# Loads of wo's pages moved behind the last stack copy, five heads later, in an Infini-attention and token-mixer kernel

## The chip, the cores and the metric

The kernel runs on one core of a Trainium2 chip. A core has five engines, each of which takes its own instructions strictly in order: TensorE (PE; its weight loads are listed apart as PEld), VectorE (DVE), ScalarE (ACT), GpSimd (POOL) and SyncE (SP), which here issues nearly all DMAs. They wait for each other by semaphores. The metric is the device time of the program in microseconds; lower is better.

## The reference

Two blocks with conditioning from a vector c: an attention over four segments of 512 tokens with a memory carried from segment to segment, and a token-mixing MLP. Cut to what is computed:

```python
mod = (_silu(c) @ w_mod).reshape(c.shape[0], 6, 1, -1)      # sa, ca, ga, sb, cb, gb
h = _layernorm(x, axis=-1) * (1 + ca) + sa
x = x + ga * _A_ref(h, A_wq, A_wk, A_wv, A_wo, A_beta)
h = _layernorm(x, axis=-1) * (1 + cb) + sb
x = x + gb * _B_ref(h, B_w1, B_b1, B_w2, B_b2)

# _A_ref: 32 heads of 32, 4 segments of 512 tokens
for s in range(N):
    logits = jnp.einsum("bhqd,bhkd->bhqk", qs, ks) * scale + mask
    a_dot = jnp.einsum("bhqk,bhkd->bhqd", _softmax(logits, axis=-1), vs)
    pq = phi(qs)
    a_mem = einsum(pq, M) / (einsum(pq, z) + 1e-6)
    outs.append(g * a_mem + (1.0 - g) * a_dot)
    M, z = M + einsum(phi(ks), vs), z + sum(phi(ks))
return o @ wo                                                # (2048, 1024) @ (1024, 1024)

# _B_ref: layernorm, u = gelu(h^T w1 + b1), y = u w2 + b2, across the tokens
```

## The kernel before

Products in full precision are made of three reduced-precision ones: an operand is kept as a high and a low part (function `split`: ACT casts the high part, another engine subtracts for the low one). A *page* is one such operand of 128 partitions, two parts of 512 columns, 512 KB, and there are 16 page buffers, taken in turn.

**Attention.** An iteration t is one group of four heads in one segment; there are 32 (`NI`), first all groups for segments 0 and 1, then all groups for segments 2 and 3, alternating between the two. Iteration 30 is the last group in segment 2, iteration 31 in segment 3. The main loop runs over n, one head at a time, and each step calls, for different heads, `scores` (logits and exponentials of head n; matmuls `a0`, `a1`, `a2`, exponentials p, their low part by POOL), `maxima` (row maxima of head n + 3; matmuls `sx`, `sy`, `sz`, then a transpose `nmps`), `values` (head n - 2; twenty matmuls `pv`), and `project` for the piece m = n + 8 of an iteration: pieces 0 and 1 are keys and values (`nps`), piece 2 transposes the keys (`kps`), makes the queries (`qps`), and writes both split into `sg`. From `sg` and from the maxima, SP copies the operands of the scores into *stacks* `sk`: three copies a head (`sk<-sg`, lines 374 to 376, function `stack`), and later four small ones for two heads (`sk<-nt`, line 493). There are two sets of four stacks, used in turn by odd and even iterations. The head outputs are transposed (`ops`), copied to `ot` and stored to `oT`.

In the second half the 16 pages hold the normalised tokens of segments 2 and 3, eight each. The loads of the sixteen pages of wo go into the same buffers, so the first eight (`wo0_0` to `wo7_0`, the columns 0 to 511 of the output) have to wait until the queries of iteration 30 are made, the others (`wo0_1` to `wo7_1`) until those of iteration 31. Three of the latter are loaded within the output product instead (line 790).

**Output product.** `product(tt)`, for 128 tokens each, loads the head outputs (`otr`), splits them into `ots`, multiplies them with wo (48 matmuls `po`, 24 for each half, line 797), adds x and stores the sum to `x1d`. Products 0 and 1 come first, their halves in turn, then 2, 3, 4, 8, 9 and so on. The MLP follows: matmuls `mx` of line 927, nearly half of the chain of waits.

**Order.** The code is traced in the order written, and a scheduler then sets each engine's order by its own estimate of times; it starts the output product while the last heads are still under way, and places `po` matmuls between theirs. `tc.issue_after(ins)` is a bound on that order: an instruction under it on the same engine's queue stands behind `ins`. It adds no wait for the end of `ins`.

Of the kernel before, what the change touches and what calls it, by code (L numbers as in the profile page):

```python
# [7 lines left out]
F32 = mybir.dt.float32  # L8
# [33 lines left out]
def attention_and_mlp(ctx, tc, x, wq, wkv, wo, beta, w1, b1, w2, b2, c, wm_a, wm_b, out):  # L42
    nc = tc.nc
    V, A, G, T, SY = nc.vector, nc.scalar, nc.gpsimd, nc.tensor, nc.sync
# [9 lines left out]
    wos = dram.tile([NK, 2, P, 2, 512], F32, name="wos")  # L54
# [86 lines left out]
    def new_page(name):  # L141
        return page.tile([P, 2, 512], F32R, tag="page", bufs=16, name=name)
# [32 lines left out]
    def load_w(g, pr):  # L175
        res = W[pr, g] = {}
        for kind, part in (("v", 0), ("v", 1), ("q", 0)):
            load_part(g, pr, kind, part, res)
        if pr == 0:
            keep_w(g)  # L180
# [176 lines left out]
    def reload_h(seg, ct):  # L357
        pg = new_page(f"h{seg}_{ct}")
        SY.dma_start(pg.bitcast(F32), hT1[seg - 2, ct])
        hpages[seg, ct] = pg  # L360

    its = [(pr, g, 2 * pr + i) for pr in range(2) for g in range(NG) for i in range(2)]
    NI = len(its)
    st = {}

    last_sk, last_nt = {}, {}
# [131 lines left out]
    @contextmanager  # L498
    def behind(n, engines):

        with ExitStack() as s:
            for e in engines:
                if (n, e) in marks:
                    s.enter_context(tc.issue_after(marks[n, e].ins))
            yield
# [92 lines left out]
    def at(f, n):  # L598
        if 0 <= n < 4 * NI:
            f(n // 4, n % 4)  # L600
# [43 lines left out]
    wop = {}  # L644
# [46 lines left out]
    for n in range(-LEADS, 4 * NI + VL):  # L691
        at(scores, n)
        at(maxima, n + LEADS)
        with behind(n, "P" if n - VL >= 64 else ""):
            at(values, n - VL)
        m = n + LEADP
        if 0 <= m + 4 < 4 * NI:
            t = (m + 4) // 4
            if its[t][:2] not in W:
                with tc.issue_after(last_sk[t - 2 if t > 16 else 0, 3].ins):  # L700
                    load_w(its[t][1], its[t][0])
        if m >= 8:
            at(project, m)
        if 59 <= m < 67:
            seg, ct = 2 + (m - 59) // 4, 2 * ((m - 59) % 4)
            with ExitStack() as s:
                if seg == 3:
                    s.enter_context(tc.issue_after((last_sk[15, 3] if ct < 4 else last_nt[14, 3]).ins))
                reload_h(seg, ct)
                reload_h(seg, ct + 1)  # L710
        if 4 * NI - 5 <= m < 4 * NI + 3:
            i = m - 4 * NI + 5
            for c in (2 * (i % 4), 2 * (i % 4) + 1):
                wop[c, i // 4] = new_page(f"wo{c}_{i // 4}")
                if c < 5 or i < 4:
                    SY.dma_start(wop[c, i // 4].bitcast(F32), wos[c, i // 4])
        for f, engines in todo.pop(n, ()):
            with behind(n, engines):
                f()
# [427 lines left out]
```

## Time and profile before

| | |
|---|---|
| median of 3 runs | 2222.85 us (2221.31 to 2225.35) |
| profiled execution | 2224.45 us, its span 2222.7 us |
| mean granted TensorE clock | 0.997 |
| PE busy | 2184.5 us, 98% |
| attention's last heads with the output product between them | about 950 to 1046 us in the span |
| output product alone | to about 1151 us, then the MLP |

A busy TensorE is the sum of what its instructions cover; idle time is shown in brackets behind the row it precedes, with the releaser. Rows of one kind that follow each other are merged, so a row's length, divided by its count, tells the pace of one. On SP a row is the issue of DMAs, not their transfer.

### The profile page before, as it was taken

How to read it: one execution, taken by the hardware profiler on the slowest of the kernel's cores; microseconds unless marked ns; L12 is line 12 of the kernel's file. 1: busy time of each engine (PE TensorE's matmuls, PEld its weight loads, DVE VectorE, ACT ScalarE, POOL GpSimd, SP SyncE). 2: the span in 40 equal slices, each digit the busy share in tenths (PEclk: the TensorE clock that was granted, in tenths of full speed). 3: DMA queues.
4: the chain of work that ended last, by engine and by line, in shares of the span. 5: the costliest groups of instructions: out<-in, count | busy, mean ns of one | idle time of the engine just before them, and what ended most of it. 6: DMA issues, size and time to landing. Idle time of an engine off the chain costs nothing.

```text
span 2222.7 us, 38130 instructions
## 1 busy us (share of the span) xinstructions
PE 2184.5 (98%) x13786; PEld 1881.3 (85%) x13786; DVE 1673.2 (75%) x3762; ACT 1132.7 (51%) x2050; POOL 723.6 (33%) x831
## 2 busy tenths in 40 slices
PE   8999999999999999999999999999999999999999
PEld 5988998889999999888888888888888888888887
DVE  7677777767777677664858766888888887869687
ACT  5476777755666666654636533533334242424232
POOL 2165766656767677553002200033330000000000
PEclk9999999999999999999999999999999999999999
DMA  7656665587566665664754686655556541414134
GB/s 287 193 172 195 183 185 160 169 297 246 167 195 203 199 206 176 192 227 133 232 204 185 227 318 255 246 225 207 214 203 222 199 153 60 142 57 147 57 124 152
DMA packets 175184, 423.05 MB, mean 190 GB/s; under 512 B 17524, under 2 KB 71828, under 8 KB 166036
## 3 DMA queue, kind: packets, MB, share of 16 engines
q1 hardware_dynamic: 174996, 420.61, 57.4%
q8 instruction: 110, 1.80, 0.3%
q14 instruction: 78, 0.64, 0.1%
HBM read 244.62 MB, written 125.06 MB: 166 GB/s over the span
## 4 chain that ended last, share of the span: by engine, by line
PE 82%; DVE 6%; DMA 5%; ACT 3%; issue 1%; POOL 1%; SPq 1%; DVEq 0%; ACTq 0%
PE mx L927 47%; PE nps L192 10%; PE qps L200 7%; PE po L797 6%; PE pv L549 3%; DMA otr<-oT 1%; PE a L515 1%; DMA sk<-sg 1%; PE sz L478 1%; PE sx L478 1%; POOL p L531 1%; PE a L522 1%; PE sy L478 1%; PE a L518 1%; PE up L460 1%
## 5 line engine op out<-in xcount | busy, mean ns | idle before, releaser
L927 PE MATMUL mx<-bU,sp 128*128 128x512 f32 x2352 | 534.7, 389 | 1.0 <-DVE ac L934 0.9
L927 PEld LDWEIGHTS mx<-bU,sp 128*128 128x128 f32 x2352 | 441.1, 188 | 94.1 <-issue 1.3
L119 ACT CAST sp<-wr 128x384 fp32r<-128x384 f32 (+2 forms) x408 | 217.2, 545 | 433.0 <-PE mx L927 354.8
L192 PE MATMUL nps<-wv,h 128*128 128x256 f32 x3072 | 430.9, 283 | 1.1 <-DVE h L122 0.7
L927 PE MATMUL mx<-bA,sp 128*128 128x512 f32 x1764 | 430.5, 389 | 0.0
L531 POOL TENSOR_TENSOR p<-p,ph 128x640 f16<-128x640 f32 x256 | 377.7, 1476 | 121.7 <-ACT ph L529 116.8
L192 PEld LDWEIGHTS nps<-wv,h 128*128 128x128 f32 x3072 | 402.7, 190 | 8.8 <-DVE h L122 1.8
L927 PEld LDWEIGHTS mx<-bA,sp 128*128 128x128 f32 x1764 | 331.2, 188 | 68.7
L122 DVE TENSOR_TENSOR sp<-wr,sp 128x384 fp32r<-128x384 f32 (+2 forms) x408 | 259.1, 646 | 28.9 <-ACT sp L119 28.7
L934 DVE TENSOR_TENSOR ac<-mx,ac 128x512 f32<-128x512 f32 x280 | 189.4, 685 | 85.1 <-PE mx L927 84.5
L200 PE MATMUL qps<-h,wq 128*128 128x512 f32 x768 | 196.4, 399 | 0.0
L529 ACT CAST ph<-p 128x1280 f16<-128x1280 f32 x128 | 161.1, 1258 | 49.7 <-POOL p L527 49.2
L797 PE MATMUL po<-wo,ots 128*128 128x512 f32 x768 | 179.7, 391 | 1.4 <-ACT ots L119 1.4
L527 POOL TENSOR_SCALAR_AFFINE_SELECT p<-p 128x256 f32<-128x256 f32 x256 | 135.5, 535 | 119.9 <-ACT p L524 70.4
L797 PEld LDWEIGHTS po<-wo,ots 128*128 128x128 f32 x768 | 143.4, 188 | 31.2 <-ACT ots L119 1.8
L927 PE MATMUL mx<-bB,sp 128*128 128x512 f32 x588 | 164.0, 389 | 0.0
L200 PEld LDWEIGHTS qps<-h,wq 128*128 128x128 f32 x768 | 140.5, 189 | 27.1
L927 PEld LDWEIGHTS mx<-bB,sp 128*128 128x128 f32 x588 | 110.4, 188 | 22.9
L934 DVE TENSOR_TENSOR cc<-mx,cc 128x512 f32<-128x512 f32 x140 | 94.9, 684 | 41.7 <-PE mx L927 41.6
L480 DVE CUSTOM_DVE_ANT_0 sz<-sz,mask 128x512 f32<-128x512 f32 x128 | 89.2, 697 | 47.8 <-PE sz L478 46.9
L480 DVE CUSTOM_DVE_ANT_0 sx<-sx,mask 128x128 f32<-128x128 f32 (+1 forms) x256 | 93.3, 365 | 35.2 <-PE sx L478 31.5
L516 ACT ACTIVATE p<-a,shift 128x512 f32<-128x512 f32 x128 | 88.0, 688 | 43.6 <-PE a L515 39.6
(207 smaller groups left out, 3193.9 us busy)
## 6 DMA issues: line engine op xcount, KB each, us to landing
sk<-sg SPq DMA_DIRECT2D x384, 128.0 KB
wr<-in_w_dram SPq DMA_DIRECT2D x28, 1024.0 KB
wr<-in_w_dram SPq DMA_DIRECT2D x32, 768.0 KB
bstu<-ucd SPq DMA_DIRECT2D x28, 768.0 KB
wsp<-wv SPq DMA_DIRECT2D x32, 512.0 KB
rawm<-in_wm_b_dram SPq DMA_DIRECT2D x32, 512.0 KB
wv<-wsp SPq DMA_DIRECT2D x32, 512.0 KB
pcd<-cc SPq DMA_DIRECT2D x14, 1024.0 KB
```

The source lines that it names most:

```text
L119: last_hi[0] = A.copy(hi, src)
L122: return lo_eng.tensor_tensor(lo, src, hi.bitcast(F32), op=ALU.subtract)
L192: T.matmul(ps[:, aa], h[:, j, 128 * tt:128 * tt + 128], wt[:, i, o:o + 256], start=(n == 0), stop=(n >= 6 * NK - 2), skip_group_check=True)
L200: T.matmul(ps, wt[:, i, o:o + 128], h[:, j], start=(k + n == 0), stop=(3 * k + n == 3 * NK - 1))
L480: marks[4 * t + h - LEADS, "V"] = V.tensor_tensor_reduce(o, o, mask[:, 384 - 128 * i:], 1.0, -3.0e38, op0=ALU.add, op1=ALU.max, accum_out= ...
L516: A.activation(p32[:, 0:512], b0, AF.Exp, scale=SCALE, bias=shift)
L527: G.affine_select(w, w, pattern=[[0, 2], [1, 128]], compare_op=ALU.is_ge, fill=0.0, base=0, channel_multiplier=-1)
L529: marks[n, "A"] = A.copy(hi, p32)
L531: marks[n, "G"] = G.tensor_tensor(lo[:, c], p32[:, c], hi[:, c], op=ALU.subtract)
L797: T.matmul(ps, os_[:, i, P * ct:P * ct + P], wop[ct, nh][:, j], start=(n == 0), stop=(n == 3 * NK - 1))
L927: T.matmul(ps, ops[q][:, i, P * k:P * k + P], b[:, j], start=(m == 0 and first), stop=(m == 3 * nk - 1), skip_group_check=True)
L934: V.tensor_tensor(d, ps, d, op=ALU.add)
```

## The change

In the main loop, the block that takes a page buffer for two blocks of wo and loads them is moved from the steps m = 123 to 130 to the steps m = 128 to 135, five heads later (piece 3 of iteration 31, which makes the last stack copies, is m = 127). Each load now stands, on SP's queue, behind the third copy to the last stack of the last segment (`last_sk[NI - 1, 3]`).

```diff
-        if 4 * NI - 5 <= m < 4 * NI + 3:
-            i = m - 4 * NI + 5
+        if 4 * NI <= m < 4 * NI + 8:
+            i = m - 4 * NI
             for c in (2 * (i % 4), 2 * (i % 4) + 1):
                 wop[c, i // 4] = new_page(f"wo{c}_{i // 4}")
                 if c < 5 or i < 4:
-                    SY.dma_start(wop[c, i // 4].bitcast(F32), wos[c, i // 4])
+                    with tc.issue_after(last_sk[NI - 1, 3].ins):
+                        SY.dma_start(wop[c, i // 4].bitcast(F32), wos[c, i // 4])
```

Nothing is added or removed: 13 loads are moved. With them the scheduler moves much of what the engines do between the end of iteration 29's heads and product 9. Lines below the edit count one more in the changed kernel (716 becomes 717, 797 becomes 798).

SP before, from the last maxima of iteration 28 on. The page `wo2_0` is the rows 256 to 383 of wo, first half of the columns; the last number of a name is a running number, and `sg30` and `sk0_0` are iteration 30's source and the first of its stacks:

```order
L493 DMA sk0_3_500<-nt1_28_3_13734 1x4x128
L716 DMA wo0_0_14141<-wos_64 128x1024
L716 DMA wo1_0_14143<-wos_64 128x1024
L716 DMA wo2_0_14263<-wos_64 128x1024
L716 DMA wo3_0_14265<-wos_64 128x1024
L716 DMA wo4_0_14381<-wos_64 128x1024
L716 DMA wo5_0_14383<-wos_64 128x1024
L781 DMA otr2_15295<-oT_57 128x8x128
L716 DMA wo6_0_14498<-wos_64 128x1024
L716 DMA wo7_0_14500<-wos_64 128x1024
L374 DMA sk0_0_497<-sg30_13999 32x2x512
```

The same place now:

```order
L493 DMA sk0_3_500<-nt1_28_3_13734 1x4x128
L782 DMA otr2_15295<-oT_57 128x8x128
L374 DMA sk0_0_497<-sg30_13999 32x2x512
L375 DMA sk0_0_497<-sg30_13999 32x2x512
L376 DMA sk0_0_497<-sg30_13999 32x1024
```

And where the pages went on SP's queue, behind the last stack of iteration 31 (`sk1_3`):

```order
L374 DMA sk1_3_504<-sg31_14437 32x2x512
L375 DMA sk1_3_504<-sg31_14437 32x2x512
L376 DMA sk1_3_504<-sg31_14437 32x1024
L717 DMA wo0_0_14630<-wos_64 128x1024
L717 DMA wo1_0_14632<-wos_64 128x1024
L717 DMA wo2_0_14697<-wos_64 128x1024
L717 DMA wo3_0_14699<-wos_64 128x1024
L493 DMA sk0_2_499<-nt0_30_3_14596 1x4x128
L493 DMA sk0_3_500<-nt0_30_3_14596 1x4x128
L493 DMA sk0_2_499<-nt1_30_3_14597 1x4x128
L493 DMA sk0_3_500<-nt1_30_3_14597 1x4x128
L717 DMA wo4_0_14765<-wos_64 128x1024
```

The first eight pages left the place ahead of iteration 30's stack copies and stand behind iteration 31's; four maxima copies of heads 2 and 3 of iteration 30 lie between the fourth and the fifth page. Between the two places, SP's queue has the copies of both iterations, two stores of `ot` and the maxima copies of heads 0 to 3 of iteration 29 and 0 and 1 of iteration 30. Behind the thirteenth page come two loads of x, the last three pages and the maxima copies of iteration 31.

TensorE before, at the end of the last projection (`qps31`):

```order
L518 MATMUL a1_29_2_14390<-sk1_2_503 128x384
L200 MATMUL qps31_14457<-h3_7_7762,wq1_7_0_1_13331 128x512 x3
L478 MATMUL sx_30_2_14520<-sk0_2_499 128x128
L478 MATMUL sx_30_2_14520<-sk0_2_499 128x256
L478 MATMUL sy_30_2_14525<-sk0_2_499 128x384
L797 MATMUL po0_0_15163<-wo0_0_14141,ots0_15144 128x512 x3
L797 MATMUL po0_0_15163<-wo1_0_14143,ots0_15144 128x512 x3
L797 MATMUL po0_0_15163<-wo2_0_14263,ots0_15144 128x512 x3
```

The same place now:

```order
L200 MATMUL qps31_14445<-h3_7_7760,wq1_7_0_1_13331 128x512 x3
L478 MATMUL sy_30_2_14509<-sk0_2_499 128x384
L478 MATMUL sz_30_2_14512<-sk0_2_499 128x512
L564 MATMUL ops28_14314<-ident_90,am28_13225 128x128 x4
L515 MATMUL a0_29_2_14375<-sk1_2_503 128x512
L518 MATMUL a1_29_2_14378<-sk1_2_503 128x384
L478 MATMUL sx_30_3_14583<-sk0_3_500 128x128
L478 MATMUL sx_30_3_14583<-sk0_3_500 128x256
L478 MATMUL sy_30_3_14588<-sk0_3_500 128x384
```

And where the first `po` stands on TensorE now:

```order
L478 MATMUL sz_31_1_14726<-sk1_1_502 128x512
L478 MATMUL sx_31_2_14787<-sk1_2_503 128x128
L478 MATMUL sx_31_2_14787<-sk1_2_503 128x256
L486 MATMUL nmps30_3_14594<-ident_90,mx30_2_14503 8x128
L522 MATMUL a2_30_1_14642<-sk0_1_498 128x256
L522 MATMUL a2_30_1_14642<-sk0_1_498 128x128
L478 MATMUL sy_31_2_14792<-sk1_2_503 128x384
L478 MATMUL sz_31_2_14795<-sk1_2_503 128x512
L478 MATMUL sx_31_3_14845<-sk1_3_504 128x128
L478 MATMUL sx_31_3_14845<-sk1_3_504 128x256
L798 MATMUL po0_0_15163<-wo0_0_14630,ots0_15144 128x512 x3
L798 MATMUL po1_0_15189<-wo0_0_14630,ots1_15153 128x512 x3
```

The output product began three rows behind the last projection; now it begins behind the scores of heads 2 and 3 of iteration 29 and 0 and 1 of iteration 30, the values of heads 0 to 2 of iteration 29, and the maxima of all heads up to the first of those of head 3 of iteration 31. From there on the products 0 and 1 take each page in turn, three matmuls each, until 82 of their 96 matmuls are ahead of the last page's; from the last of product 9's first half on, TensorE's order is the same in both kernels.

## The prediction

> **What bounds the kernel now.** I read the page first, then the busy time by stretches around the end of attention, then TensorE's and SP's order in time there, and the chain of waits. The page says that TensorE is the bound nearly everywhere:
>
> ```profile
> PE 2184.5 (98%) x13786; PEld 1881.3 (85%) x13786; DVE 1673.2 (75%) x3762; ACT 1132.7 (51%) x2050; POOL 723.6 (33%) x831
> PE 82%; DVE 6%; DMA 5%; ACT 3%; issue 1%; POOL 1%; SPq 1%; DVEq 0%; ACTq 0%
> ```
>
> So the change costs or gains what it adds to or takes from TensorE's idle time. The stretches show how little there is to take (the columns: stretch, its length, then PE busy; behind POOL stand the granted clock, the DMA share and GB/s):
>
> ```profile
> 920.00:940.00 20.00, 18.89 (x177) 18.22 (x177) 13.19 (x44) 11.86 (x21) 12.02 (x14) 1.00 0.83 255
> 940.00:960.00 20.00, 19.92 (x150) 17.05 (x150) 11.53 (x38) 13.69 (x24) 11.95 (x18) 1.00 0.75 221
> 960.00:980.00 20.00, 19.34 (x147) 16.25 (x147) 11.93 (x47) 8.27 (x13) 13.12 (x16) 1.00 0.45 156
> 980.00:1000.00 20.00, 19.79 (x125) 16.52 (x124) 13.46 (x35) 11.21 (x21) 9.86 (x11) 1.00 0.83 277
> 1020.00:1040.00 20.00, 18.63 (x132) 14.84 (x131) 6.65 (x18) 4.80 (x8) 7.51 (x8) 1.00 0.50 166
> 1040.00:1060.00 20.00, 20.00 (x92) 16.52 (x91) 10.79 (x27) 7.80 (x16) 0.46 (x1) 1.00 0.44 146
> ```
>
> From 920 to 1040 the idle parts are 1.11, 0.08, 0.66, 0.21 and 1.37 us (the stretch 1000 to 1020 is full): 3.4 us. From 1040 on PE is full. TensorE's order is the same in both kernels up to 930.6 us and again from product 9 on, so 3.4 us, 0.15%, is about all that the change can win.
>
> Where the loads stand in time, on SP's queue (start, length, line):
>
> ```profile
> 915.53 3.11 SPq L716 DMA_DIRECT2D wo<-wos  x6
> 919.22 4.94 SPq L716 DMA_DIRECT2D wo<-wos  x2
> 924.25 0.68 SPq L374 DMA_DIRECT2D sk<-sg  x1
> 951.49 0.68 SPq L374 DMA_DIRECT2D sk<-sg  x1
> 952.21 0.63 SPq L375 DMA_DIRECT2D sk<-sg  x1
> 961.33 2.62 SPq L493 DMA_DIRECT2D sk<-nt  x4
> 965.46 0.59 SPq L376 DMA_DIRECT2D sk<-sg  x1
> ```
>
> The eight pages of the first half of wo go out from 915.5 on, in front of segment 2's stack copies (924.25); segment 3's twelve copies run from 951.49 to 965.46. TensorE at the two places that matter:
>
> ```profile
> 930.64 0.45 PE L192 MATMUL nps<-wv,h 128*128 128x256 f32 x2
> ...
> 935.11 0.47 PE L478 MATMUL sx<-sk 96*128 96x128 f32 x2 [1.08 <-DMA sk<-sg]
> ...
> 948.84 0.47 PE L515 MATMUL a<-sk 98*128 98x512 f32 x1
> 949.14 0.34 PE L518 MATMUL a<-sk 98*128 98x384 f32 x1
> 949.32 0.85 PE L200 MATMUL qps<-h,wq 128*128 128x512 f32 x3
> 950.01 0.39 PE L478 MATMUL sx<-sk 96*128 96x128 f32 x2
> 950.42 4.94 PE L797 MATMUL po<-wo,ots 128*128 128x512 f32 x21
> ...
> 1028.36 3.98 PE L797 MATMUL po<-wo,ots 128*128 128x512 f32 x15 [1.37 <-ACT ots L119]
> ```
>
> The last projection ends at 950.0 and 0.4 us later the output product (po) starts. It is the filler between the heads' short matmuls from there on, and it needs the pages.
>
> **What it removes.** Segment 2's copies no longer stand behind 4 MB of pages. In the chain of waits the copies that were caught behind them took 9.20 us to land, and in a quiet place 2.29:
>
> ```profile
> 925.77 9.20 DMA sk<-sg
> 317.11 2.29 DMA sk<-sg
> 735.96 3.86 DMA rawm<-in_wm_b_dram
> ```
>
> The wait behind them was the 1.08 us at 935.11. I credit all 3.4 us of idle time, since the 1.37 at 1028 (the product waits for ots, which is split from the heads' stored outputs) also goes when the heads run ahead of the product; that is the generous side.
>
> **What it adds.** (a) The last projection ends earlier. From 930.64, the last common row, to its end at 950.0 PE spent 19.4 us, of which 1.1 were idle (the 1.08 above) and 0.5 (948.84 to 949.32) went to two score matmuls that now stand behind it, while 0.2 of maxima moved ahead: 18.0 us, so it ends near 948.6.
>
> (b) SP's queue then stands between that end and the first page. Before, the first copy went out 1.5 us after the projection's end, at 951.49; I take 1.0, as ACT, which was late there, has less ahead of it: 949.6. In front of the first page now stand twelve copies, one store of ot and four copies of nt: 12 x 0.64 + 0.4 + 2.6 = 10.7 us, so the first page is issued at 960.3. A 512 KB load took 3.86 us to land (the rawm row above): 964.2. From 948.6 that is 15.6 us.
>
> (c) What TensorE has to do meanwhile is only heads. Their cost, start to start:
>
> ```profile
> 967.22 0.48 PE L549 MATMUL pv<-vp,p 128*128 128x65 bf16 x10
> 967.53 0.60 PE L549 MATMUL pv<-vp,ph 128*128 128x97 bf16 x10
> 967.95 0.48 PE L478 MATMUL sz<-sk 96*128 96x512 f32 x1
> 968.27 0.40 PE L515 MATMUL a<-sk 98*128 98x512 f32 x1
> 968.51 0.39 PE L478 MATMUL sx<-sk 96*128 96x128 f32 x2
> 968.74 0.34 PE L518 MATMUL a<-sk 98*128 98x384 f32 x1
> 968.92 0.27 PE L486 MATMUL nmps<-ident,mx 128*8 128x128 f32 x1
> 995.10 5.39 PE L797 MATMUL po<-wo,ots 128*128 128x512 f32 x23
> ```
>
> Values of a head 0.73; scores (a, 512, 384 and twice up to 256 wide) 0.24 + 0.18 + 0.18 = 0.6; maxima (sx, and sy and sz, which are as wide as the first two of a) 0.24 + 0.18 + 0.24 = 0.66; a po matmul 5.39 / 23 = 0.23. In the changed order there stand between the last qps and the first po four heads' scores (2.4), five heads' worth of maxima (3.3), three heads' values (2.2) and about 1.3 of transposes and memory reads (eight matmuls and more of 128 columns): 9.2 us. Idle: 15.6 - 9.2 = 6.4 us. These heads are hidden behind nothing, and each copy waits its turn: with 2.29 us to land the third stack of segment 3 is there near 960.5, so the idle time comes in pieces.
>
> (d) The rest of the pages come in one burst. How fast, the DMA's rate in 40 slices of 4.1 us from 880 to 1045 shows:
>
> ```profile
> GB/s 347 235 235 74 218 160 179 98 43 338 399 337 227 161 97 129 258 312 231 68 65 297 378 0 64 287 366 382 240 131 127 0 122 20 182 127 107 151 254 133
> ```
>
> 338, 399 and 337 are the eight pages: 358 GB/s, 1.46 us for one. The last page of the second half, with two loads of x among them, is the 18th: 964.2 + 17 x 1.46 = 989.0. Ahead of its use stand 82 po matmuls (19.0) and, by the same prices, 4.4 us of heads: 23.4 of 24.8 us, idle 1.4. SP's issue, 3.11 / 6 = 0.52 us a page, lies beside that, and so do the four nt copies (2.6 us) that stand between the fourth page and the fifth. Behind the burst on SP wait the nt copies of segment 3; the first scores that need them stand behind the 82 po matmuls, so they cost nothing unless those are done sooner. The last three pages of the second half stay where they were, behind the two loads of x.
>
> (e) The clock. Where PE idled in pieces this kernel lost clock as well:
>
> ```profile
> 130.00:140.00 10.00, 7.20 (x50) 6.61 (x51) 9.36 (x13) 6.94 (x11) 7.59 (x6) 0.83 1.01 297
> 490.00:500.00 10.00, 7.32 (x47) 6.21 (x46) 6.80 (x18) 6.25 (x12) 7.24 (x8) 0.73 0.97 358
> 500.00:510.00 10.00, 10.00 (x88) 9.55 (x88) 7.20 (x15) 5.56 (x10) 5.53 (x6) 0.93 0.72 168
> 495.10 0.51 PE L549 MATMUL pv<-vp,p 128*128 128x65 bf16 x6 [1.38 <-POOL p L531]
> 495.42 1.20 PE L200 MATMUL qps<-h,wq 128*128 128x512 f32 x2
> ```
>
> 2.7 us of idle in 490 to 500, with short matmuls of values between, were followed by a clock of 0.73 and 0.93 in ten microseconds each: 2.7 + 0.7 = 3.4 us of lost clock (two qps take 1.20, where three took 0.85 at 949.32). At 130 to 140 it was 1.7. The 1.08 at 935 cost none. So the bounds are 0 and 3.4; the stretch of (c), also idle in pieces between heads, is nearest to the one at 490, so I take 3.4, lost after the first page has come. It fills the 1.4 of (d) first, which is then no idle any more.
>
> [...]
>
> **Sum.** +6.4 (first page) + 3.4 (clock, which covers the 1.4) - 3.4 (idle time of before) = +6.4 us. The profiled execution took 2224.45 us for its span of 2222.7; the median of the runs is 2222.85, inside 0.1% of it. Forecast on the median: 2229.2 us; the same sum on the profiled execution would give 2230.9. No instruction is added, and everything behind product 9 only moves later by the same amount.
>
> **Rivals.**
> *The heads gain what the copies gain (not slower).* The copies of segments 2 and 3 come out from behind the pages, the heads run ahead, and the pages still arrive before TensorE has run dry. It decides at 948.6 + 9.2 = 957.8: a first page by then leaves no idle, and 3.4 us are won: 2219.5 us. For it speaks the 9.20 us row; against it, that SP alone needs 10.7 us before it issues that page.
> *It costs little.* The clock holds, as after the 1.08 us at 935, and the queue and landing are each half a microsecond to a microsecond shorter: 5.0 + 1.4 - 3.4 = +3.0, 2225.8 us. For it speaks that the stretch keeps TensorE six tenths busy.
> *The burst is the bound.* The pages share the DMA with the stack copies, x and stores, and come at the 277 GB/s of the 980 to 1000 stretch: 1.9 us each, so the 18th lands at 996, and idle in (d) is 8.9 instead of 1.4: 6.4 + 8.9 - 3.4 = +11.9, 2234.8 us; with the clock falling again more. For it speaks the 9.20 us that small copies wait behind such a burst, since the nt copies for segment 3 now stand in it; against it the 358 GB/s.
>
> **Chances.** The forecast 0.55 (its own range 2226.5 to 2232), the burst 0.18, little 0.20, the gain 0.07. The measurement tells about 0.2%, 4.4 us, from no change: slower begins at 2227.3. Of the forecast's 0.55 some 0.47 lie above it, and all of the burst: slower 0.65. The gain's 3.4 us is within 0.2%, so faster needs something that the trace doesn't show: 0.03. The rest, 0.32, is the same. Range for 8 in 10: from 2224, below the cheap case, to 2236, above the burst.
>
> **What would show it.** In the changed profile, PE busy should fall to about nine of fifteen microseconds right before the first po, which starts near 964 instead of 950.4; the first page's issue should follow the last segment's twelfth copy on SP; the granted clock should dip below 1 around 960 to 975; the 1.08 us wait of sx for sk should be gone. I am wrong if po starts before 958, if PE idles again behind the first pages (the burst), or if the idle time of 1020 to 1040 remains.

## The result, and the profile after

The changed kernel took 2234.79 us (median of six runs, 2230.44 to 2236.43), the kernel before 2224.10 us on the same chip: a ratio of 1.0049 [1.0038, 1.006], so 10.7 us slower. Run once more on another chip, beside two of the experiments, it took 2231.3 us against 2222.93: 1.0041 [1.0029, 1.0053], 8.4 us. It is slower, as forecast, and inside the range, but above the forecast's own 2226.5 to 2232 in the first set; the size was 6.4 us and came out at 8.4 to 10.7.

The page of the changed kernel, busy time and granted clock in 40 slices:

```profile
PE 2190.9 (98%) x13786; PEld 1884.4 (84%) x13786; DVE 1671.8 (75%) x3762; ACT 1132.2 (51%) x2050; POOL 723.8 (32%) x831
PEclk9999999999999999989999999999999999999999
```

TensorE is *busier* by 6.4 us than before, with the same 13786 matmuls: work that ran at a lower clock took longer and counts as busy (ten `pv` take 1.01 us instead of 0.60 below). One slice of the clock has an 8, and it holds the end of attention. The stretches there (PE busy is the first number behind the stretch's length; the granted clock, the DMA share and GB/s are the last three; the last row sums the eight stretches from 920 to 1080):

```profile
920.00:940.00 20.00, 20.00 (x207) 19.64 (x205) 14.88 (x51) 14.22 (x24) 13.08 (x17) 1.00 0.41 93
940.00:960.00 20.00, 17.98 (x139) 15.11 (x138) 14.17 (x52) 13.54 (x27) 13.14 (x19) 0.89 0.32 74
960.00:980.00 20.00, 18.80 (x123) 15.09 (x123) 8.39 (x34) 7.46 (x11) 11.19 (x13) 0.85 0.94 331
980.00:1000.00 20.00, 18.04 (x98) 14.57 (x95) 6.97 (x20) 6.81 (x12) 7.89 (x10) 0.91 0.57 214
1020.00:1040.00 20.00, 20.00 (x140) 16.40 (x139) 12.85 (x30) 9.08 (x15) 9.99 (x9) 1.00 0.37 124
sum 160.00, PE 154.60 PEld 130.33 DVE 90.57 ACT 78.64 POOL 65.97; mean PE 19.33 PEld 16.29 DVE 11.32 ACT 9.83 POOL 8.25
```

The same sum of the kernel before, whose clock was 1.00 in all eight stretches:

```profile
sum 160.00, PE 156.57 PEld 133.05 DVE 97.70 ACT 85.34 POOL 66.14; mean PE 19.57 PEld 16.63 DVE 12.21 ACT 10.67 POOL 8.27
```

Idle time went from 160 - 156.57 = 3.43 us to 5.40, which is 2.0 us. The larger part is clock: (0.11 + 0.15 + 0.09) x 20 = 7.0 us that TensorE lost, where it lost none before. Together 9.0 us, beside 9.9 us between the two spans (2232.6 and 2222.7). A lost clock counted this way is an upper figure, since a part may fall into idle time.

TensorE in order of time:

```profile
942.72 5.74 PE L200 MATMUL qps<-h,wq 128*128 128x512 f32 x24
948.30 0.34 PE L478 MATMUL sy<-sk 96*128 96x384 f32 x1
...
953.90 0.47 PE L478 MATMUL sx<-sk 96*128 96x128 f32 x2 [1.34 <-DMA sk<-sg]
...
955.83 0.76 PE L515 MATMUL a<-sk 98*128 98x512 f32 x1 [0.61 <-ACT p L524]
...
957.41 1.01 PE L549 MATMUL pv<-vp,ph 128*128 128x97 bf16 x10
...
964.41 0.44 PE L478 MATMUL sy<-sk 96*128 96x384 f32 x1 [0.78 <-DVE mx L480]
965.26 0.50 PE L478 MATMUL sz<-sk 96*128 96x512 f32 x1 [0.41 <-DVE mx L480]
965.78 0.79 PE L478 MATMUL sx<-sk 96*128 96x128 f32 x2
...
985.74 10.28 PE L798 MATMUL po<-wo,ots 128*128 128x512 f32 x37 [1.96 <-DVE x L801]
```

The last projection ends at 948.5. From then to the first `po`, at 966.37 right behind the `sx` of 965.78, TensorE has heads alone. It never stands idle for long: the longest piece is 1.34 us. From 955.83 on, though, ten `pv` take 1.01 us instead of 0.60 and a score 0.76 instead of 0.47. The last row is a second hole, 20 us later.

SP's queue, the first page's issue and the burst behind it:

```profile
949.11 0.68 SPq L374 DMA_DIRECT2D sk<-sg  x1
...
960.30 1.44 SPq L376 DMA_DIRECT2D sk<-sg  x1
961.78 2.02 SPq L717 DMA_DIRECT2D wo<-wos  x4
964.83 2.62 SPq L493 DMA_DIRECT2D sk<-nt  x4
967.49 5.98 SPq L717 DMA_DIRECT2D wo<-wos  x9
973.52 1.83 SPq L787 DMA_DIRECT2D x<-in_x_dram  x2
976.29 2.88 SPq L791 DMA_DIRECT2D wo<-wos  x3
```

The two loads of x go out behind thirteen pages. VectorE adds x to each finished half of a product, and by that frees the bank that TensorE needs for a later half. The waits between 945 and 1000 (in total, times, longest), and VectorE's rows at the second hole:

```profile
PE po L798 <- DVE x L801: 2.0, 1, 2.0
PE sx L478 <- DMA sk<-sg: 1.3, 1, 1.3
DVE x L801 <- DMA x<-in_x_dram: 0.6, 1, 0.6
```

```profile
983.29 0.28 DVE L489 SCALAR_TENSOR_TENSOR nt<-nmps,nt 8x128 fp32r<-8x128 f32 x1 [1.52 <-ACT nt L488]
983.82 0.19 DVE L552 RECIPROCAL pv<-pv 128x4 f32<-128x4 f32 x1 [0.25 <-PE pv L549]
...
984.71 0.35 DVE L556 SCALAR_TENSOR_TENSOR red<-red,gate,pv 128x128 f32<-128x128 f32 x1
984.98 0.69 DVE L801 SCALAR_TENSOR_TENSOR x<-po,x 128x512 f32<-128x512 f32 x1
...
986.28 0.69 DVE L801 SCALAR_TENSOR_TENSOR x<-po,x 128x512 f32<-128x512 f32 x1 [0.59 <-DMA x<-in_x_dram]
```

The addition that TensorE waits for, at 984.98, follows VectorE's work on a head without a pause. Only the second one waits for x, and by then TensorE is running again (985.74). So what holds TensorE in the second hole is VectorE's order, in which the addition stands behind work for the last heads, and not the landing of x.

### The profile page after: what moved, and what is told of

It reads as the page before. It is cut to its first block, busy times and chain, and to the rows that moved or that the text cites. A ratio compares the mean times of both kernels' runs of the same rounds, so it can differ in the third digit from the quotient of the medians.

```text
span 2232.6 us, 38132 instructions
## 1 busy us (share of the span) xinstructions
PE 2190.9 (98%) x13786; PEld 1884.4 (84%) x13786; DVE 1671.8 (75%) x3762; ACT 1132.2 (51%) x2050; POOL 723.8 (32%) x831
## 4 chain that ended last, share of the span: by engine, by line
PE 82%; DVE 8%; DMA 4%; ACT 3%; issue 1%; POOL 1%; SPq 1%; DVEq 0%; ACTq 0%
PE mx L928 45%; PE nps L192 11%; PE po L798 7%; PE qps L200 7%; PE pv L549 3%; DMA wr<-in_w_dram 1%; PE a L515 1%; PE sx L478 1%; PE sz L478 1%; PE a L522 1%; PE a L518 1%; DVE ac L935 1%; PE sy L478 1%; DVE wv L122 1%; DMA rawm<-in_wm_b_dram 1%
```

## The experiments

Eleven runs were made, each compared with the kernel before on its own chip. The theory: the loss is idle time in pieces and, above all, the clock that these pieces bring down. The rivals: the pages come too late whatever the clock does, the five heads matter, or TensorE has no room.

**1. Only the five heads, not the queue place.** The loads at the late steps, without the bound on SP's order:

```diff
                 if c < 5 or i < 4:
-                    with tc.issue_after(last_sk[NI - 1, 3].ins):
-                        SY.dma_start(wop[c, i // 4].bitcast(F32), wos[c, i // 4])
+                    SY.dma_start(wop[c, i // 4].bitcast(F32), wos[c, i // 4])
```

> One part alone: the loads stand five heads later in the code, without the order behind the last stack copy. Theory (it is the place on SP's queue behind segment 3's copies that costs): the order of every engine is that of before, so within 0.2% of before, near 2224 us, first po near 950 us and no dip of the clock there. Rival (the five heads cost, since the page buffers are taken later): slower by a part of the 10.7 us, 2227 to 2234 us.

Measured: 2223.63 us, ratio 0.9999 [0.9988, 1.0011]. Every engine's order is that of the kernel before, row for row: the scheduler puts the loads where they were. So the five heads in the code do nothing, and the place on SP's queue is the whole change.

**2. The same queue place one segment earlier.** The loads in their old steps, bound behind the last stack copy of iteration 30 instead of 31:

```diff
-                    SY.dma_start(wop[c, i // 4].bitcast(F32), wos[c, i // 4])
+                    with tc.issue_after(last_sk[NI - 2, 3].ins):
+                        SY.dma_start(wop[c, i // 4].bitcast(F32), wos[c, i // 4])
```

> The loads stand where they stood before, but each behind the last stack copy of iteration 30 instead of 31. It takes segment 2's copies out from behind the pages as the change does, and leaves the pages ahead of segment 3's. Theory: pages are there when the last projection ends, so first po near 949 us, no idle in pieces after it and a clock of 1.0; the 1.08 us wait of before is gone: 2221 to 2225 us. Rival (any order that puts the pages behind stack copies costs, because eight pages then delay the following small copies): 2228 us or more, with PE waiting for sk.

Measured: 2224.2 us, ratio 1.0003 [0.9993, 1.0013]. The stretches 920 to 960 are full and the first `po` stands behind the last projection (952.50), but new idle pieces come between 960 and 980, two of them in the second fence:

```profile
940.00:960.00 20.00, 20.00 (x147) 17.62 (x146) 12.10 (x41) 10.79 (x20) 9.83 (x15) 1.00 0.98 355
960.00:980.00 20.00, 18.75 (x159) 15.57 (x158) 11.70 (x47) 10.59 (x15) 13.75 (x18) 1.00 0.66 209
```

```profile
970.37 0.49 PE L478 MATMUL sx<-sk 96*128 96x128 f32 x2 [0.46 <-DVE rdd L453]
974.52 3.69 PE L798 MATMUL po<-wo,ots 128*128 128x512 f32 x15 [0.80 <-DVE x L801]
```

Idle falls to 1.63 us between 920 and 1080, yet the time does not fall measurably. Freeing the copies of segment 2 is worth at most about 2 us.

**3. Only the second half of wo late.** The first eight pages as before, the others behind the last stack copy:

```diff
-        if 4 * NI - 5 <= m < 4 * NI + 3:
-            i = m - 4 * NI + 5
+        if 4 * NI - 5 <= m < 4 * NI - 1 or 4 * NI + 4 <= m < 4 * NI + 8:
+            i = m - 4 * NI + 5 if m < 4 * NI - 1 else m - 4 * NI
...
+                    with ExitStack() as s:
+                        if i >= 4:
+                            s.enter_context(tc.issue_after(last_sk[NI - 1, 3].ins))
+                        SY.dma_start(wop[c, i // 4].bitcast(F32), wos[c, i // 4])
```

> One part of the change: the first eight pages stand as before, only the second half's go five heads later and behind the last stack copy of segment 3. Theory (the first half's lateness leaves TensorE without filler): products 0 and 1 start near 950 us as before, 48 matmuls fill the stretch; most of the 10.7 us is gone: 2223 to 2227 us. Rival (the burst of late pages and what stands behind it on SP, the x loads and maxima copies, is the cost): 2229 to 2235 us, with PE idle when the second half begins.

Measured: 2229.89 us, ratio 1.0026 [1.0014, 1.0038]: more than the theory said, so it fell here. With the first half in time the first `po` is at 948.08, as early as it can be, and the loss comes twenty microseconds later in the same two forms:

```profile
960.00:980.00 20.00, 16.72 (x121) 13.05 (x120) 14.46 (x57) 8.61 (x13) 11.48 (x14) 0.83 0.83 297
```

```profile
971.12 0.51 PE L478 MATMUL sz<-sk 96*128 96x512 f32 x1 [1.12 <-DVE mx L480]
975.79 5.39 PE L800 MATMUL po<-wo,ots 128*128 128x512 f32 x15 [0.78 <-DVE x L803]
```

The last heads' maxima stand in a row with no `po` between them, each waiting for VectorE; 3.3 us are idle, the clock is 0.83 (3.4 us), and fifteen `po` take 5.39 us, 0.36 each instead of 0.23. So the loss doesn't need a late first page: a stretch of heads without enough `po` between them was enough here. The rival's 2229 to 2235 us held, and so did its idle piece where the second half begins (0.78 us). TensorE's rows show no wait for a page there, however, and the addition that ends that piece came right behind a maximum of the heads, without a wait for x.

**4 and 5. x ahead of the last pages.** In the changed kernel, seven pages instead of three are left to the output product, behind the loads of x:

```diff
-                if c < 5 or i < 4:
+                if c < 1 or i < 4:
...
-                for c in range(5, NK):
+                for c in range(1, NK):
```

> The changed kernel, with the loads of x for products 0 and 1 ahead of the last seven pages instead of the last three. TensorE's order is nearly the same and the first po comes as late. In the changed kernel PE idled 1.96 us at 984 us until DVE had emptied a bank of po, which needs x, and the clock fell once more (0.91 from 980 to 1000). Theory (that second hole costs about 2 us of idle and 1.8 of clock): 2230 to 2232 us. Rival (the clock would have been low there anyway, or the pages behind x become late instead): 2234 to 2236 us.

Measured: 2231.32 us, ratio 1.0037 [1.0023, 1.0051], inside the theory's range, which looked like the 2 to 3 us of the second hole. It ran again, beside the changed kernel and with its trace:

> The changed kernel itself, beside the next two on the same chip, so that these are compared with it directly: 2233 to 2236 us.

> The rows x of the first two products ahead of the last seven pages, once more, for its trace. Theory: the hole of 2.0 us before the third half product (PE waits for VectorE, which waits for x) and the half-speed stretch behind it, 1.8 us, are gone between 980 and 1000, the clock between 950 and 970 is as low as in the changed kernel: 3 to 4 us under it, 2230 to 2232 us. Rival (the hole only moves, since the pages come later by as much): the time of the changed kernel within 1 us.

Measured: changed 2231.3 us, where 2233 to 2236 had been expected; x ahead 2233.36 us (2230.28 to 2238.07), ratio 1.0052 [1.0038, 1.0066]. In the second comparison it is no faster than the changed kernel (2.1 us slower, with intervals that overlap), so the theory's 2230 to 2232 us was missed and the gain of the first comparison isn't established. The rival, that the hole only moves, stands in substance, though its number (within 1 us) wasn't met either. The trace (of an execution at 2231.14 us) shows the move: the stretch from 980 is full, since VectorE's order changed with the loads and its first addition now stands at 981.63, but the idle time is elsewhere.

```profile
960.00:980.00 20.00, 17.86 (x120) 14.21 (x119) 8.11 (x34) 7.36 (x12) 11.23 (x14) 0.91 0.94 335
980.00:1000.00 20.00, 20.00 (x134) 16.61 (x132) 7.85 (x23) 9.54 (x15) 10.16 (x13) 1.00 0.67 239
1000.00:1020.00 20.00, 19.03 (x122) 15.79 (x121) 10.75 (x26) 12.88 (x25) 12.10 (x13) 1.00 0.78 273
```

```profile
981.63 0.69 DVE L801 SCALAR_TENSOR_TENSOR x<-po,x 128x512 f32<-128x512 f32 x1
```

**6. Fillers.** The experiment that tells clock and room apart: matmuls whose results nobody uses, four (or eight) in each of the six heads after the last projection, added to the changed kernel. Nothing of the computation is left out.

```diff
+        if 4 * NI <= m < 4 * NI + 6:
+            wq_ = W[its[NI - 1][:2]]["q", 0]
+            fl = bank("pj", 2, f"fill{m}")
+            for j in range(4):
+                T.matmul(fl, wq_[:, 0, 0:128], wq_[:, 1], start=True, stop=True, skip_group_check=True)
```

> The changed kernel with 24 more matmuls (four in each of the six heads after the last projection, a page of wq's against itself, the results used by nobody): 24 x 0.235 us = 5.6 us of added TensorE work where its pieces of idle time and its halved clock stood, 948 to 966 us. Theory (the changed kernel loses its time to the idle pieces and to the clock that they bring down, not to a lack of room): the fillers take the 2.0 us of idle time between 940 and 960 and keep the clock at full speed there, so that of the 5.2 us lost to both between 940 and 980 as much comes back as they cost: 2229 to 2235 us, no slower than the changed kernel, with a granted clock over 0.95 between 940 and 965. Rival (the work after the last projection is bound by when the pages arrive or by TensorE itself): the fillers are added whole, 2234.8 + 5.6 = 2240 us.

> The same with eight matmuls in each of the six heads: 48 x 0.235 = 11.3 us of added TensorE work. Theory: about 5 us of it come back, 2238 to 2242 us; the granted clock stays at full speed until the first product. Rival (all of it added): 2246 us. If it is no slower than with four, TensorE has more free room there than its rows show.

> Control: the same 24 fillers in the kernel before, whose TensorE has no idle piece and no lost clock between 940 and 1000. Both theories: added whole, 2223.5 + 5.6 = 2229 us. If it costs under 3 us, the fillers are not worth 5.6 us and the two runs with fillers must be read by what this one costs.

Measured: with 24 fillers 2230.27 us, 1.0034 [1.0022, 1.0046]; with 48, 2232.69 us, 1.0045 [1.0032, 1.0058]; the control, 24 fillers in the kernel before, 2226.9 us, 1.0013 [0.9999, 1.0026]. The two rivals' 2240 and 2246 us are refuted: compared through the kernel before, 5.6 us and even 11.3 us of added TensorE work cost the changed kernel (1.0049 and 1.0041) nothing that can be measured. The theory's own 2238 to 2242 us for 48 fillers was missed too: it expected about 5 us to come back, and in the traces 4.3 us of idle time (5.40 to 1.10) and all 7.0 us of lost clock did, which is what the fillers cost. In the kernel before the same 24 cost 3.9 us, with an interval that holds both nothing and their full price, so the control by itself decides little; the traces carry the reading. The trace with 24 fillers:

```profile
940.00:960.00 20.00, 19.83 (x149) 16.93 (x148) 14.20 (x51) 12.84 (x22) 12.66 (x20) 1.00 0.39 91
960.00:980.00 20.00, 18.26 (x138) 14.90 (x134) 9.02 (x33) 8.19 (x14) 10.43 (x14) 1.00 1.00 384
980.00:1000.00 20.00, 18.05 (x111) 15.07 (x108) 6.60 (x19) 6.93 (x12) 7.93 (x11) 1.00 0.64 215
```

```profile
940.90 5.74 PE L200 MATMUL qps<-h,wq 128*128 128x512 f32 x24
...
947.29 0.68 SPq L374 DMA_DIRECT2D sk<-sg  x1
...
959.26 3.82 SPq L717 DMA_DIRECT2D wo<-wos  x7
963.19 1.66 PE L803 MATMUL po<-wo,ots 128*128 128x512 f32 x6 [1.11 <-DMA wo<-wos]
...
981.84 0.68 DVE L806 SCALAR_TENSOR_TENSOR x<-po,x 128x512 f32<-128x512 f32 x1
982.58 8.66 PE L803 MATMUL po<-wo,ots 128*128 128x512 f32 x37 [1.95 <-DVE x L806]
```

The clock stays at 1.00 from 920 to 1080. The first page is issued at 959.26 instead of 961.78, but most of these 2.5 us are older: the last projection ended 2.0 us sooner in this execution (946.48 instead of 948.46), which lost no clock at 130 to 140, where that of the changed kernel lost 1.7. From SP's first copy to the first page it is 12.0 us here (947.29 to 959.26) and 12.7 in the changed kernel, so the heads at full speed brought the page only 0.7 us closer. Now a real wait for the page is seen, 1.11 us, and the page landed 963.19 - 959.26 = 3.9 us after its issue. By the same 3.9 us, which is an estimate, the changed kernel's first page landed near 965.7, while the last heads were still under way: TensorE's rows there show no wait for a page, and the first `po` at 966.37 came right behind the heads. The second hole is as long as before (1.95 us), and here no addition waits for x at all.

**7. Two combinations.** The second half late with x ahead (edits 3 and 4), and 24 fillers with x ahead (edits 6 and 4):

> First eight pages where they were before, the second eight behind the last copy, and the loads of the rows x for the first two products ahead of the last seven pages in place of the last three. Theory (in the run with the second half late the products' eviction waited for x behind thirteen pages, and the idle pieces brought the clock to 0.83 between 960 and 980): the wait for x goes, 0.8 us and a part of the 3.4 us of lost clock, 2225 to 2228 us. Rival (the clock falls by the idle pieces between the last heads, whatever x does): 2229 to 2231 us, as with the second half late.

> Both: x ahead of the last seven pages, and 24 filler matmuls (5.6 us) in the six heads after the last projection. Theory (two separate losses): under the run with the fillers alone (2230.3) by the 2.0 us of the hole, and under x ahead alone in spite of 5.6 us more work: 2227 to 2230 us, granted clock 1.0 from 900 to 1080. Rival (one loss, counted twice): no less than the smaller of the two, 2230 to 2232 us.

Measured: 2228.02 us, 1.0022 [1.0011, 1.0032], at the theory's edge and below the rival, though its interval meets that of experiment 3; and 2229.13 us, 1.0035 [1.0023, 1.0047], within the theory's numbers and 2.2 us under the changed kernel in the same comparison, with 5.6 us more work; it is 1.1 us under the fillers alone, where 2.0 were expected. In the first the loss moved once more: from 1000 to 1020 TensorE is idle for 2.8 us and the clock is 0.83. The second has the clock at 1.00 from 920 to 1080 and 3.07 us of idle time. No run points to a version faster than the kernel before.

**The accounts side by side.** For each profiled execution, from 920 to 1080: idle time (160 less the summed PE), lost clock (what is missing to 1 in each stretch, times 20), added work; their sum less the 3.43 us of before, and the difference of medians.

| kernel | idle | lost clock | added work | sum against before | measured |
|---|---|---|---|---|---|
| changed | 5.40 | 7.0 | | +9.0 | +10.7 |
| changed, again | 5.90 | 7.0 | | +9.5 | +8.4 |
| behind iteration 30 | 1.63 | 0 | | -1.8 | +0.9 |
| second half late | 4.43 | 3.4 | | +4.4 | +6.6 |
| second half late, x ahead | 4.92 | 3.4 | | +4.9 | +5.1 |
| x ahead (second set) | 4.85 | 3.6 | | +5.0 | +10.4 |
| 24 fillers | 3.85 | 0 | 5.6 | +6.0 | +7.3 |
| 48 fillers | 1.10 | 0 | 11.3 | +9.0 | +9.7 |
| 24 fillers, x ahead | 3.07 | 0 | 5.6 | +5.2 | +6.2 |
| before with 24 fillers | 1.92 | 1.6 | 5.6 | +5.7 | +3.9 |

Idle time, lost clock and added work account for nine of ten rows within 2.7 us. The exception is x ahead, whose profiled execution was among its quicker ones; the granted clock of its runs, over the whole span, goes from 0.994 to 0.997. Each sum comes from one execution. Outside 920 to 1080 these executions lost between 3.4 and 10.4 us of clock, all of it before 840 us, so the time of a single one says little about this stretch, and the sums stand beside medians.

## Why the prediction was right, and where its sizes were off

**What is removed: right, worth little.** The 1.08 us wait of `sx` for `sk` is gone (920 to 940 is full), and so is the 1.37 us at 1028 (1020 to 1040 is full). Experiment 2 has the first of these gains without the price, and measures no faster.

**(a) and (b): right but for the last link.** The last projection ended at 948.5, forecast 948.6; the first copy went out at 949.11, forecast 949.6; the first page at 961.78, forecast 960.3; the first `po` at 966.37, forecast 964.2. SP needed 12.7 us from the first copy to the first page, forecast 10.7: its rows add up to 11.3 us of issue, and the rest are pauses between them. One link failed, though: the gap didn't end with the page. The page was there near 965.7 (the estimate above), and the first `po` came behind the heads, which the clock had stretched. Page and heads were done within a microsecond of each other, so it is partly luck that the page's forecast landing lies so near the first `po`.

**(c): the gap right, its form not.** The gap is 17.9 us, forecast 15.6:

```profile
948.46:966.37 17.91, 14.69 (x111) 11.67 (x110) 15.11 (x56) 12.81 (x22) 11.11 (x15) 0.79 0.63 166
```

Idle in it is 3.2 us, not 6.4; lost clock is 0.21 x 17.91 = 3.8 us. Together 7.0 us, and 14.69 - 3.8 = 10.9 us of work at full speed, forecast 9.2; that work is moved here from elsewhere and is no loss. I had put all of it down as idle time and the fall of the clock after it, "lost after the first page has come". The clock fell inside the gap, and stretched the heads that fill it. That the gap cost 7.0 us where 6.4 were forecast is luck in part: idle time that was put too high and lost clock that was put elsewhere nearly cancel.

**(d): the burst right, the second hole missed.** The DMA's rate from 880 to 1045 in slices of 4.1 us:

```profile
GB/s 306 292 218 81 219 158 173 115 13 120 191 159 6 95 4 3 1 162 118 154 306 377 321 417 409 409 143 1 153 276 387 207 347 159 82 121 122 254 77 209
```

306 to 417 while the pages come: the rival with 277 GB/s is refuted in its mechanism, although its 2234.8 us is the time that was measured first. Behind the first `po`, 2.0 us of idle time came all the same, near the 1.4 of the step but for another reason: TensorE waited for a bank that VectorE freed late (1.96 us at 985.74), because VectorE's addition stood behind its work for the last heads. The step had no term for VectorE's order. The hole doesn't depend on the landing of x, since it is as long with 24 fillers, where no addition waits for x. With x ahead VectorE adds earlier and this hole is gone, but nothing that held up was gained (experiments 4 and 5), since idle time came back at other places.

**(e): the term that was mis-sized.** I took 3.4 us of lost clock, which "fills the 1.4 of (d) first, which is then no idle any more". It was 7.0 us in all: 3.8 in the gap (where it stands in for forecast idle time) and 3.2 behind it, and it covered nothing: idle pieces of 1.96 and 0.23 us stand beside it. So behind the first `po` 5.4 us were lost where 3.4 were forecast, and in the gap 7.0 where 6.4 were: 6.4 + 2.0 + 0.6 = 9.0 us, the sum above. What is left to 10.7 is no more than the two sets of runs differ by (8.4 and 10.7).

Ahead of the clock's fall in the gap the longest idle piece was 1.34 us. How much idle time brings the clock down, no run shows.

## What to carry to other kernels

Queue loads behind small copies only if the tensor engine has other dense work until the loads land: a stretch of short, dependent matmuls cost twice here, in the gap of 17.9 us once as idle pieces (3.2 us) and again as a lower clock (0.79, 3.8 us), which showed as busy time and not as idle. A hole that was closed in such a stretch came back elsewhere here; what held the clock up was dense work (1.00 from 920 to 1080 with 24 fillers in the changed kernel). And take out one half of an edit first: here the move in the code did nothing, and the bound on the queue did everything.

## What was not expected of the hardware

Lost clock came in lumps: 3.4, 3.4, 3.6, 7.0, 7.0 and 1.6 us in the six executions above that lost any, all near multiples of 1.7. Counted in stretches of 10 us instead of 20, the same six are 3.4, 3.4, 3.4, 6.8, 6.8 and 1.7 us.

Equal idle time didn't always bring the clock down. The hole before the third half product was 1.96 us in the changed kernel, and the clock fell behind it (0.91 over 980 to 1000); with 24 fillers it was 1.95 us at the same place, and the clock stayed at 1.00. Far from the change, where the two kernels don't differ, the kernel before had a clock of 0.83 with 7.20 of 10 us busy; the execution with 24 fillers had less busy time and no loss, although a part of the 7.20 is work that the low clock itself stretched:

```profile
130.00:140.00 10.00, 6.79 (x56) 5.80 (x56) 9.36 (x16) 8.06 (x14) 7.82 (x7) 1.00 1.02 304
```

What decides between the two was not settled.
